# A squared-relu layer by seven block products over chunk pairs, the last stage so for all row pairs, and an issue order from tables

## The chip, the cores and the metric

The kernel runs on one core of one Trainium2 chip. The metric is device microseconds of one execution. Before the change three runs gave 356.97, 357.52 and 357.94; the median is **357.52 us**.

## The reference, cut to what matters

Three layers follow each other on a batch of 2 sequences of 768 rows, 512 features: a local attention with block summaries (8 heads), a mixture of 4 attention experts of which the best 2 count, and a layer with a squared relu and a gate. The change touches the third most:

```python
def _moe2_ref(x, mu_k, mu_r, w_k, w_v, w_r):
    x_prev = np.concatenate([np.zeros((B, 1, D)), x[:, :-1, :]], axis=1)
    xk = mu_k * x + (1.0 - mu_k) * x_prev
    xr = mu_r * x + (1.0 - mu_r) * x_prev
    k = np.maximum(xk @ w_k, 0.0)          # 512 -> 1024, the hidden layer
    v = k * k @ w_v                        # 1024 -> 512
    r = 1.0 / (1.0 + np.exp(-(xr @ w_r)))  # the gate
    return r * v
```

w_k, w_v and w_r come as 64-bit floats, which the chip unpacks from integer words.

## The kernel before

Every matmul of two dense operands is done with operands split into a rounded part and a remainder ("halves"), as three products: rounded x rounded, rounded x remainder, remainder x rounded. Rounding is one instruction of ScalarE, VectorE or GpSimd (`rnd`, lines 699 to 702), the remainder one subtraction of VectorE or GpSimd (`sub`, 707 and 709).

The 1536 rows are worked in 4 chunks of 384 (two for each sequence). Stage 1 (`stage1_*`) is the local attention by tiles of 128 rows; `proj_all` (products of line 1077 and 1095) and `attention` (1177 scores, 1237 transposes, 1263 weighted values, 1305 output projection) are the experts by chunk. Then for the last layer: `mix` makes xk or xr of a chunk in halves (line 1424 is its multiply-add), `rec` is the gate (1442: 12 matmuls of 512 columns for each of 12 row tiles, then Sigmoid at 1451), `hid` the hidden layer (1466: for each chunk 8 groups of 128 hidden columns, each 4 pieces of the contraction x 3 matmuls of 384 columns; then Relu on ScalarE at 1471 and a multiply out of PSUM on VectorE at 1472). The last stage works on tiles of 128 rows. `mono(t)` does one tile by plain block products; `duo(ta, tb)` does two tiles by seven block products (2 x 2 blocks over row tile and hidden half, and hidden half and output half), with sums and differences of the blocks made by VectorE or GpSimd (`add`, 1371 and 1372). Each block product is 12 matmuls of 256 columns (1513). `ALONE = 2` tiles go through `mono`, ten through `duo`. Weights are loaded by `load_wr`, `load_wk`, `load_wv`, each 128 rows through `raw64` (1348 to 1357: two words to one 32-bit float).

The order of all work is set when the program is built. Each instruction, or small group, is an `op` with the tiles that it reads and writes and up to four "ways" (engines). `Plan.run` gives each a rank (its distance to the end by cost formulas, plus an entry of the table `RANKS`), and `Plan.simulate` places them one by one on model clocks of the engines with biases from `LEANS` and `ENGINE_BIAS`; the resulting order is what every engine's queue gets. Tiles come from small pools by name (`x`, `pq0`, `wx`, `stage`, ...), PSUM has six shared banks `ps` and one each of `a1` and `a2`. From the middle on, weight pieces are put into tiles of earlier stages that are done (`parts`).

Of the kernel before, what the change touches and what calls it, by code (L numbers as in the profile page):

```python
# [58 lines left out]
ALONE = 2

RANKS = (
# [1716 lines left out]
```

## Time and profile before

| what | value |
|---|---|
| runs | 356.97, 357.52, 357.94 us |
| span of the profiled execution, first to last instruction | 356.0 us |
| time of the profiled execution beside its span | not recorded apart; the median of the runs is 1.5 us above the span |
| TensorE busy | 340.2 us (96%), 3084 matmuls |
| VectorE busy | 290.5 us (82%), 878 instructions |
| ScalarE busy | 215.6 us (61%), 597 |
| GpSimd busy | 115.9 us (33%), 128 |
| granted TensorE clock | 1.000 |
| DMA | 33.89 MB, mean 95 GB/s |

A busy time is the time in which at least one instruction of the engine runs; instructions of one engine overlap a little, so counts times means are more than busy time. Matmuls are shown with a duration of some twice their pitch, because the next one starts before the last has ended; the pitch is read from unbroken runs.

### The profile page before, as it was taken

How to read it: one execution, taken by the hardware profiler on the slowest of the kernel's cores; microseconds unless marked ns; L12 is line 12 of the kernel's file. 1: busy time of each engine (PE TensorE's matmuls, PEld its weight loads, DVE VectorE, ACT ScalarE, POOL GpSimd, SP SyncE). 2: the span in 40 equal slices, each digit the busy share in tenths (PEclk: the TensorE clock that was granted, in tenths of full speed). 3: DMA queues.
4: the chain of work that ended last, by engine and by line, in shares of the span. 5: the costliest groups of instructions: out<-in, count | busy, mean ns of one | idle time of the engine just before them, and what ended most of it. 6: DMA issues, size and time to landing. Idle time of an engine off the chain costs nothing.

```text
span 356.0 us, 8257 instructions
## 1 busy us (share of the span) xinstructions
PE 340.2 (96%) x3084; PEld 307.2 (86%) x3084; DVE 290.5 (82%) x878; ACT 215.6 (61%) x597; POOL 115.9 (33%) x128
## 2 busy tenths in 40 slices
PE   3979979999999999999999999999999999999996
PEld 2769967888878899888878898999999898999995
DVE  3897778999999899899997799999995266326994
ACT  1888757999888555786678367775740333522440
POOL 0345030034410534445625532063224351601113
PEclk9999999999999999999999999999999999999999
DMA  7997847646130132102211310100002000000112
GB/s 267 384 356 216 286 135 227 225 141 192 46 124 3 59 119 80 40 2 94 84 61 59 101 56 30 53 1 17 29 32 100 5 0 0 2 0 2 59 47 73
DMA packets 19206, 33.89 MB, mean 95 GB/s; under 512 B 2112, under 2 KB 9024, under 8 KB 19168
## 3 DMA queue, kind: packets, MB, share of 16 engines
q1 hardware_dynamic: 19168, 33.38, 28.2%
q8 instruction: 24, 0.39, 0.5%
q14 instruction: 14, 0.11, 0.1%
HBM read 29.63 MB, written 3.15 MB: 92 GB/s over the span
## 4 chain that ended last, share of the span: by engine, by line
PE 61%; DVE 1%; issue 0%
PE ps L1466 19%; PE ps L1513 17%; PE ps L1442 9%; PE ps L1305 4%; PE a L1263 3%; PE ps L1237 3%; PE ps L1077 2%; PE ps L1177 2%; PE ps L1095 2%; DVE kw L707 0%; PE ps L1218 0%; DVE pq L1184 0%; DVE wvgl L1538 0%; DVE wvgl L1371 0%; DVE gl L1102 0%
## 5 line engine op out<-in xcount | busy, mean ns | idle before, releaser
L1197 ACT ACTIVATE pq<-pq,nm 128x128 f32<-128x128 f32 (+5 forms) x48 | 31.7, 661 | 10.6 <-DVE nm L1184 8.6
L1351 POOL TENSOR_SCALAR f<-f 128x512 f32<-128x512 f32 x13 | 23.8, 1834 | 33.1 <-ACT f L1348 31.1
L1077 PE MATMUL ps<-x,wqkh 128*128 128x384 f32 x128 | 34.2, 348 | 0.0
L1184 DVE CUSTOM_DVE_ANT_0 pq<-ps,trm 128x384 f32<-128x384 f32 (+3 forms) x64 | 29.7, 501 | 1.3 <-PE ps L1177 1.3
L944 ACT ACTIVATE pp<-pp,nm 128x120 f32<-128x120 f32 x72 | 27.4, 383 | 0.4 <-DVE nm L941 0.4
L1237 PE MATMUL ps<-cst,pq 128*128 128x128 f32 x168 | 25.0, 275 | 0.0
L1077 PEld LDWEIGHTS ps<-x,wqkh 128*128 128x128 f32 x128 | 22.1, 189 | 0.7
L1095 PE MATMUL ps<-wvgh,x 128*128 128x260 f32 x96 | 21.7, 300 | 0.1
L1077 PE MATMUL ps<-x,wqkl 128*128 128x384 f32 x64 | 21.5, 335 | 0.0
L1466 PE MATMUL ps<-x,wqkh 128*128 128x384 f32 x96 | 21.4, 338 | 0.0
L1237 PEld LDWEIGHTS ps<-cst,pq 128*128 128x128 f32 x168 | 19.5, 141 | 1.9 <-issue 0.9
L1263 PE MATMUL a<-th,vv 128*64 128x384 f32 (+2 forms) x144 | 20.6, 421 | 0.0
L1177 PE MATMUL ps<-ks,q 64*128 64x384 f32 (+3 forms) x192 | 20.3, 338 | 0.0
L1472 DVE SCALAR_TENSOR_TENSOR q<-ps,q 128x384 f32<-128x384 f32 x16 | 8.5, 556 | 13.9 <-ACT q L1471 13.8
L1466 PE MATMUL ps<-x,wqkl 128*128 128x384 f32 x96 | 19.4, 337 | 0.0
L699 ACT ACTIVATE th<-ps 128x384 f32<-128x384 f32 (+1 forms) x37 | 16.7, 482 | 3.8 <-PE ps L1237 2.7
L1442 PE MATMUL ps<-vw,x 128*128 128x512 f32 x72 | 18.7, 395 | 0.0
L1348 ACT ACTIVATE f<-stage 128x512 f32<-128x512 f32 x20 | 13.5, 682 | 8.5 <-DVE th L707 3.0
L1177 PEld LDWEIGHTS ps<-ks,q 64*128 64x128 f32 x192 | 15.1, 185 | 3.9 <-issue 1.0
L1095 PEld LDWEIGHTS ps<-wvgh,x 128*128 128x128 f32 x96 | 16.1, 188 | 1.8 <-issue 1.2
L941 DVE CUSTOM_DVE_ANT_0 pp<-ps,msk 128x120 f32<-128x120 f32 x72 | 15.8, 275 | 1.9 <-PE ps L918 1.8
L1466 PEld LDWEIGHTS ps<-x,wqkh 128*128 128x128 f32 x96 | 17.1, 188 | 0.0
(324 smaller groups left out, 1074.7 us busy)
## 6 DMA issues: line engine op xcount, KB each, us to landing
stage<-in_wk SPq DMA_DIRECT2D x8, 512.0 KB, 3.5
stage<-in_wv SPq DMA_DIRECT2D x8, 512.0 KB, 3.9
qb<-in_qT SPq DMA_DIRECT2D x12, 256.0 KB, 5.0
out_y<-wvgl SPq DMA_DIRECT2D x24, 128.0 KB, 1.7
vw<-in_vp SPq DMA_DIRECT2D x8, 256.0 KB, 4.1
stage<-in_wr SPq DMA_DIRECT2D x4, 512.0 KB
kw<-in_kS SPq DMA_DIRECT2D x6, 320.0 KB
ks<-in_kS SPq DMA_DIRECT2D x4, 400.0 KB, 5.3
```

The source lines that it names most:

```text
L944: op("act", act(NK, True) + 186, lambda i=i, z=z, pr=pr, nm=nm: nc.scalar.activation(pr()[:, i], pr()[:, i], AF.Exp, bias=nm.t[:, i:i + 1] ...
L1077: mm(p.t[:, :C], a.t[:, kc, cols], x.t[:, kc, :], start=(kc == 0 and i == 0), stop=(kc == KC - 1 and i == 2))
L1095: mm(p.t[:, :260], x.t[:, kc, tok], a.t[:, kc, :], start=(kc == 0 and i == 0), stop=(kc == KC - 1 and i == 2))
L1177: mm(ps[e2].t[:, :z - a], q1.t[r, x, tok], ks.t[r, y, a:z], start=n == 0, stop=n == 2)
L1184: nc.vector.tensor_tensor_reduce(pr.t[:, a:z], p.t[:, :z - a], trm.t[:, 512 - nk + a:512 - nk + z] if z == nk and not a else (trm.t[:, 512 ...
L1197: nc.scalar.activation(pr.t[:, :nk], pr.t[:, :nk], AF.Exp, bias=nm.t[:, m:m + 1], scale=-1.0, accum_out=sme.t[:, k, i, 0:1]), r=[nm, (sme, ...
L1237: lambda i=i, kb=kb, pr=pr: nc.tensor.transpose(p.t[:, i * P:(i + 1) * P], pr.t[:, kb * P:(kb + 1) * P], ident()),
L1263: mm(acc.t[64 * e2:64 * e2 + 64, tq0 * P:(tq0 + cnt) * P], vv.t[:, kb, e * D:(e + 1) * D], th[e2].t[:, i0 * P:(i0 + cnt) * P], start=first ...
L1351: ("pool", pool_ts(512), lambda: nc.gpsimd.tensor_scalar(ff(), ff(), F64_TOP, None, ALU.min))],
L1442: mm(p.t, a.t[:, kc, tok], w[2](), start=(kc == 0 and i == 0), stop=(kc == KC - 1 and i == 2))
L1466: mm(p.t[:, :C], w[2]()[:, mo:mo + P], a.t[:, kc, :], start=(kc == 0 and i == 0), stop=(kc == KC - 1 and i == 2))
L1513: mm(p.t[:, :256], x.t[:, u, j * P:(j + 1) * P], v[2]()[:, col:col + 256], start=(at == 0 and i == 0), stop=(at == n - 1 and i == 2))
```

## The change

The hidden layer is done for two chunks at a time (`hid(0)`, `hid(2)`), by the scheme that `duo` had: blocks of the contraction (two halves of the 512 features) and of the rows (two chunks), against blocks of w_k by contraction half and column parity of 256-column pieces. Seven block products take the place of eight; each has four groups of 128 hidden columns with 6 matmuls of 384 columns. Sums and differences of weight blocks are made at load time (`seven`, now shared by w_k and w_v), those of inputs between the products (`into`), those of results after them (`copy`, `plus`, `plus_in`, `more`), and the squared relu follows as its own step on a result in SBUF (`square`). `mono` goes; all twelve row tiles go through `duo` in six pairs, where the first and second product's results are now copied out of PSUM. The gate's steps are the same. Pools are merged by size (`w`, `b6`, `s4`, `t`, ...), all eight PSUM banks are shared. The planner's simulation is gone: `ORDER` is a list of 2151 numbers, entry n issues operation n // 4 done its (n % 4)th way, and `HOMES` gives each tile its slot. The clipping of unpacked weights on GpSimd gets a second operation (times 1.0). Copies of value sums into the value tiles can be done by any engine or by a DMA.

```diff
-RANKS = (
...
-LEANS = {
...
+ORDER = (
+    12, 4, 0, 8, 24, 16, 44, 36, 52, 32, 60, 56, 28, 68, 20, 64, 220, 48, 172, 40, 72, 193, 76, 260, 672, 224, 678,
+    236, 80, 264, 834, 228, 268, 84, 272, 88, 360, 836, 244, 232, 92, 252, 1297, 184, 256, 308, 276, 284, 280, 188,
...
+HOMES = (
+    0, 0, 16, 0, 0, 0, 0, 0, 0, 0, 0, 0, 1, 3, 4, 1, 2, 0, 2, 5, 6, 7, 0, 1, 15, 26, 0, 1, 2, 3, 19, 20, 23, 24, 21,
...
+        assert len(ORDER) == len(self.ops) and len(HOMES) == len(self.bufs)
+        for b, home in zip(self.bufs, HOMES):
+            b.slot = home
+        issued = set()
+        for n in ORDER:
+            o = self.ops[n // 4]
+            assert o.preds <= issued
             for b in o.bufs:
                 if b.tile is None:
                     b.tile = alloc(b)
...
+            o.ways[n % 4][2]()
+            issued.add(o)
...
-    banks = {"ps": 6, "a1": 1, "a2": 1}
+    banks = {"ps": 8}
+    kinds = dict(w=39, u3=5, p1=3, t=8, q=8, b6=10, s4=6)
     slots = dict(
-        cst=1, msk=1, trm=1, mu=1, omu=1, wqkh=1, wqkl=1, wvgh=1, wvgl=1, woh=1, wol=1, x2=3, qb=NQ, kw=2, vw=4,
-        f64=2, oh=1, ol=1, ksm=1, vs=1, x=4, nm=8, sms=1, rss=1, sme=1, rse=1, ks=1, vv=1, q1=2, gl=2, gate=2, cc=1, cnt=1, gsum=1, mx=1,
-        fs=1, pq0=3, pq1=3, pq2=3, nm2=10, wx=8, **SLOTS, **banks,
+        cst=1, msk=1, mu=1, omu=1, ksm=1, ks=1, nm=8, sms=1, rss=1, sme=1, rse=1, gl=2, gate=2, cc=1, cnt=1, gsum=1,
+        mx=1, nm2=10, **kinds, **banks,
     )
-    plan = Plan(slots, ("ps",), banks)
+    plan = Plan(slots, ("ps", *kinds), banks)
     buf, op = plan.buf, plan.op
...
-            if t >= PUT:
-                op("sp", dma(NB * 2048, 255.0), lambda v=v, s2=s2: nc.sync.dma_start(v.t[SROW[s2]], vsm[b].t[:NB]),
-                   r=[vsm[b]], w=[(v, "sum")])
-                continue
...
+                ("sp", dma(NB * 2048, 255.0), lambda v=v, s2=s2: nc.sync.dma_start(v.t[SROW[s2]], vsm[b].t[:NB])),
+            ], r=[vsm[b]], w=[(v, "sum")], issue=850)
...
-                       ("pool", pool_ts(512), lambda: nc.gpsimd.tensor_scalar(ff(), ff(), F64_TOP, None, ALU.min))],
+                       ("pool", pool_ts(512), lambda: nc.gpsimd.tensor_scalar(
+                           ff(), ff(), F64_TOP, 1.0, ALU.min, ALU.mult))],
...
+    def seven(fa, fb, sums, homes):
+        w = [part("q", 256), part("q", 256)] + homes
+        for i, (x, y, fn) in enumerate(sums):
+            both("dve", at(*x), at(*y[:3]), at(*y[3:]), 256, fn, [(fa, 0), (fb, 0), (fa, 1), (fb, 1)][:2 + i // 2],
+                 [(x[0], 1)])
+        halves(w[0], w[1], at(fa, 0, 0), [(fa, 0)], 256)
+        halves(w[2], w[3], at(fb, 0, 0, 512), [(fb, 0)])
+        halves(w[4], w[5], at(fa, 1, 0, 512), [(fa, 1)])
+        halves(w[6], w[7], at(fb, 1, 0, 512), [(fb, 1)])
+        return w
+    def load_wk():
+        cols = wk.rearrange("k (m c) -> k m c", m=2)
+        for n in range(4):
+            g, j = divmod(n, 2)
+            fa, fb = (raw64(cols[k * P:(k + 1) * P, :, 256 * g:256 * g + 256], 2) for k in (j, j + 2))
+            a11, a21, a12, a22 = (fa, 0, 0), (fa, 0, 256), (fb, 0, 0), (fb, 0, 256)
+            s1, s2, s3, s4 = (fa, 1, 0), (fa, 1, 256), (fb, 1, 0), (fb, 1, 256)
+            homes = pieces("s4", 2, 512) if n < 2 else [part("w"), part("w")]
+            homes += [part("w"), part("w")] + [part(("w", "w", "w", "u3")[n]) for x in range(2)]
+            wkp[g, j] = seven(fa, fb, ((s1, a21 + a22, ALU.add), (s2, s1 + a11, ALU.subtract),
+                                       (s3, a11 + a21, ALU.subtract), (s4, a12 + s2, ALU.subtract)), homes)
...
+    def mixed(c, i, kc):
+        piece = part("t", C, F32)
+        mb, mk, tmp = piece
+        def cur():
+            return x2s[c].t[:, kc, 1:]
+        def prv():
+            return x2s[c].t[:, kc, 0:C]
+        rd = [(x2s[c], kc), (x2s[c], "prev"), mu, omu]
+        mul_by("pool", tmp, prv, lambda: omu.t[:, i:i + 1], C, rd, [(mb, mk)])
+        op("dve", dve(C) + 60, lambda: nc.vector.scalar_tensor_tensor(
+            tmp(), cur(), mu.t[:, i:i + 1], tmp(), ALU.mult, ALU.add), r=rd, w=[(mb, mk)], lock=True)
+        return piece
...
+    def blocks(c):
+        if c:
+            return [pieces("b6", 4, C, F32) for i in range(2)]
+        b = buf("ks", [P, FC, C])
+        return [[(b, i, lambda i=i: b.t[:, i]) for i in range(4 * h, 4 * h + 4)] for h in range(2)]
+    def copy(x, p, n):
+        rnd("act", x[2], lambda: p.t[:, :n], n, [p], [x[:2]])
+    def plus(x, p, n):
+        op("dve", dve(n), lambda: nc.vector.tensor_tensor(x[2](), p.t[:, :n], x[2](), ALU.add), r=[p], w=[x[:2]])
+    def hid(c):
+        (c11, c21), (c12, c22) = k2s[c], k2s[c + 1] = blocks(c), blocks(c + 1)
+        b11, b21, b12, b22 = ([mixed(c + cc, kc, kc) for kc in (2 * kh, 2 * kh + 1)]
+                              for cc in range(2) for kh in range(2))
+        def split(x):
+            o = buf("b6", [P, 2, 2, C], F32R)
+            for j in range(2):
+                halves(*((o, (u, j), lambda u=u, j=j: o.t[:, u, j]) for u in range(2)), x[j][2], [x[j][:2]], C)
+            return o
+        def into(dst, x, y):
+            for j in range(2):
+                both("dve", dst[j][2], x[j][2], y[j][2], C, ALU.subtract, [x[j][:2], y[j][:2]], [dst[j][:2]])
+        def product(m, x, w, col):
+            g, o = divmod(m, 2)
+            o = col + o * P
             p = bank("ps")
+            def go():
+                for j in range(2):
+                    h, l = wkp[g, j][2 * w:2 * w + 2]
+                    for i, (a, u) in enumerate(((h, 0), (h, 1), (l, 0))):
+                        mm(p.t[:, :C], a[2]()[:, o:o + P], x.t[:, u, j], start=not (j or i), stop=j == 1 and i == 2)
+            op("pe", 6 * pe_r(C), go, r=[x] + [v[:2] for j in range(2) for v in wkp[g, j][2 * w:2 * w + 2]], w=[p],
+               stream="p3")
+            return p
+        def square(x):
+            any_of("act", [
+                ("dve", dve(C) + 60, lambda: nc.vector.scalar_tensor_tensor(
+                    x[2](), x[2](), 0.0, x[2](), ALU.max, ALU.mult), True),
+                ("act", 2 * act(C, True), lambda: (nc.scalar.activation(x[2](), x[2](), AF.Relu),
+                                                   nc.scalar.activation(x[2](), x[2](), AF.Square))),
+                ("pool", pool_ts(C) + pool_tt(C), lambda: (
+                    nc.gpsimd.tensor_scalar(x[2](), x[2](), 0.0, 1.0, ALU.max, ALU.mult),
+                    nc.gpsimd.tensor_tensor(x[2](), x[2](), x[2](), ALU.mult))),
+            ], w=[x[:2]])
+        def plus_in(dst, p, x):
+            op("dve", dve(C), lambda: nc.vector.tensor_tensor(dst[2](), p.t[:, :C], x[2](), ALU.add), r=[p, x[:2]],
+               w=[dst[:2]])
+        def more(x, y):
+            both("dve", x[2], x[2], y[2], C, ALU.add, [y[:2]], [x[:2]])
+        four = range(4)
+        x = split(b11)
+        for m in four:
+            copy(c11[m], product(m, x, 0, 0), C)
+        into(b11, b12, b11)
+        x = split(b11)
+        for m in four:
+            copy(c22[m], product(m, x, 2, 0), C)
+        into(b11, b22, b11)
+        x = split(b11)
+        for m in four:
+            plus_in(c12[m], product(m, x, 2, 256), c11[m])
+        x = split(b21)
+        for m in four:
+            plus(c11[m], product(m, x, 1, 0), C)
+            square(c11[m])
+        into(b12, b22, b12)
+        x = split(b12)
+        for m in four:
+            plus_in(c21[m], product(m, x, 3, 0), c12[m])
+            more(c12[m], c22[m])
+            more(c22[m], c21[m])
+            square(c22[m])
+        into(b21, b21, b11)
+        x = split(b21)
+        for m in four:
+            plus(c21[m], product(m, x, 1, 256), C)
+            square(c21[m])
+        x = split(b22)
+        for m in four:
+            plus(c12[m], product(m, x, 3, 256), C)
+            square(c12[m])
...
+        (cb, ck, ca), (db, dk, da) = part("u3", dt=F32), part("u3", dt=F32)
+        s, d = (flat(ca), [(cb, ck)]), (flat(da), [(db, dk)])
+        p1 = kept(product(operand(a11), 0, 0))
+        add(s, a21, a22, ALU.add)
+        p5 = kept(product(operand(s), 2, 0))
+        add(s, s, a11, ALU.subtract)
+        u2 = plus_to(product(operand(s), 2, 256), p1)
+        plus(p1, product(operand(a12), 1, 0), 256)
+        result(ta, 0, p1)
+        add(d, a11, a21, ALU.subtract)
+        u3 = plus_to(product(operand(d), 3, 0), u2)
+        more(u2, p5)
+        more(p5, u3)
+        result(tb, 256, p5)
+        plus(u3, product(operand(a22), 3, 256), 256)
+        result(tb, 0, u3)
+        add(s, a12, s, ALU.subtract)
+        plus(u2, product(operand(s), 1, 256), 256)
+        result(ta, 256, u2)
...
+    rg, k2s = [], {}
+    rec(0, mix(0))
+    load_wk()
     attention(3)
+    rec(1, mix(1))
+    hid(0)
+    hid(2)
+    rec(2, mix(2))
+    rec(3, mix(3))
+    load_wv()
+    for t in range(0, B * TPB, 2):
+        duo(t, t + 1)
     plan.run(alloc)
```

## Rows read from the trace of the kernel before

**Rows 1.** Busy us and instructions (x) of each engine in eight stretches, with TensorE clock.
```profile
core 0: us, PE busy (x) PEld busy (x) DVE busy (x) ACT busy (x) POOL busy (x), PEclk, DMA share, GB/s
0.00:20.00 20.00, 12.52 (x275) 10.36 (x276) 12.32 (x63) 11.31 (x49) 4.54 (x15) 1.00 0.93 334
20.00:60.00 40.00, 35.35 (x505) 31.31 (x503) 32.62 (x142) 29.55 (x111) 12.06 (x14) 1.00 0.72 230
60.00:120.00 60.00, 60.00 (x750) 49.20 (x750) 58.44 (x236) 54.31 (x188) 15.18 (x18) 1.00 0.38 121
120.00:177.00 57.00, 56.88 (x421) 50.47 (x417) 52.06 (x154) 34.55 (x87) 27.50 (x30) 1.00 0.23 75
177.00:241.00 64.00, 64.00 (x364) 57.70 (x361) 59.20 (x141) 44.77 (x90) 22.83 (x19) 1.00 0.15 50
241.00:272.40 31.40, 31.40 (x267) 31.40 (x266) 28.59 (x58) 14.95 (x28) 9.36 (x8) 1.00 0.11 36
272.40:322.70 50.30, 50.30 (x267) 47.17 (x266) 21.39 (x39) 15.70 (x31) 16.99 (x18) 1.00 0.03 10
322.70:356.00 33.30, 29.77 (x253) 29.56 (x251) 25.91 (x54) 10.44 (x18) 7.47 (x8) 1.00 0.14 48
sum 356.00, PE 340.21 PEld 307.16 DVE 290.53 ACT 215.59 POOL 115.94; mean PE 42.53 PEld 38.40 DVE 36.32 ACT 26.95 POOL 14.49
```

**Rows 2.** Chain that ended last: start us, length us, engine, tile, line, count.
```profile
224.37 16.83 PE ps L1466 x96
241.20 31.21 PE ps L1513 x264
272.41 8.33 PE ps L1442 x36
...
352.50 0.43 DVE wvgl L1538
...
352.96 0.42 DVE wvgl L1371
```

**Rows 3.** All products of two lines: the hidden stage's, then the last stage's.
```profile
...
187.40:322.80 135.40, 68.75 (x384) 67.10 (x383) 1.00 0.10 32
...
0.00:356.00 356.00, 61.29 (x516) 61.22 (x516) 1.00 0.29 95
```

**Rows 4.** Timeline of TensorE (start, length): products that follow four transposes at 147.04.
```profile
147.39 0.42 PE L1305 MATMUL ps<-oh,woh 128*128 128x384 f32 x1
147.65 0.34 PE L1305 MATMUL ps<-ol,woh 128*128 128x384 f32 x1
```

**Rows 5.** Four kinds of VectorE instructions: duration ns, least/median/most.
```profile
L1424 DVE SCALAR_TENSOR_TENSOR ol<-x,mu,ol x24: 603/608/1373, 207.7 to 301.6; 128x384 f32<-128x384 f32 x24
...
L1355 DVE SCALAR_TENSOR_TENSOR f<-stage,f x20: 678/684/1462, 67.5 to 228.6; 128x512 int32<-128x512 int32 x20
...
L707 DVE TENSOR_TENSOR x<-ol,x x19: 544/550/1112, 210.2 to 305.1; 128x384 fp32r<-128x384 f32 x19
L707 DVE TENSOR_TENSOR f<-wx,f x8: 676/681/689, 247.8 to 346.7; 128x512 fp32r<-128x512 f32 x8
```

**Rows 6.** Timeline of VectorE: two instructions that follow each other.
```profile
204.64 0.43 DVE L1371 TENSOR_TENSOR f<-f,f 128x256 f32<-128x256 f32 x1
204.98 0.42 DVE L700 CAST wx<-f 128x512 fp32r<-128x512 f32 x1
```

**Rows 7.** Groups by line and shape: busy us, mean ns, idle before.
```profile
L1424 DVE SCALAR_TENSOR_TENSOR ol<-x,mu,ol 128x384 f32<-128x384 f32 x24 | 15.3, 654 | 2.1 <-POOL ol L716 2.1
L707 DVE TENSOR_TENSOR f<-wx,f 128x512 fp32r<-128x512 f32 x8 | 5.5, 682 | 0.0
...
L1351 POOL TENSOR_SCALAR f<-f 128x512 f32<-128x512 f32 x13 | 23.8, 1834 | 33.1 <-ACT f L1348 31.1 <-DVE nm L1184 1.9
...
L1451 ACT ACT_TABLE_LOAD x1 | 1.3, 1283 | 0.0
```

**Rows 8.** Waits of TensorE before 60 us: us, times, longest.
```profile
PE ps L923 <- DMA ks<-in_kS: 5.0, 1, 5.0
PE a L1002 <- ACT ks L699: 2.3, 1, 2.3
```

More of the change, by code (lines that the diff above doesn't have):

```diff
@@ L381 @@
 class Op:
[L382 to L383 removed]
+    pass
 class Plan:
[L395 to L402 removed]
@@ L403 @@
-    HOLD = dict(pe=200.0, act=225.0, dve=200.0, pool=135.0, sp=1150.0)
-    TICK, BUSY = 10240.0 / 3, 3060.0
-    MODES = ("full", "rows", "half", "quarter")
-    SWITCH = {}
-    for a in MODES:
-        for b in MODES:
-            SWITCH[a, b] = 95.0
     def __init__(self, slots, shared, banks):
         self.slots, self.shared, self.banks = slots, shared, banks
-        self.ops, self.order, self.chain = [], {p: [] for p in slots}, {}
-        self.n, self.tilt = 0, 0.0
+        self.ops, self.order, self.bufs, self.chain = [], {p: [] for p in slots}, [], {}
@@ L417, in buf, with op @@
     def buf(self, pool, shape, dt=F32):
-        self.n += 1
-        b = Buf(pool, shape, dt, f"{pool}_{self.n}")
+        b = Buf(pool, shape, dt, f"{pool}_{len(self.bufs) + 1}")
+        self.bufs.append(b)
         self.order[pool].append(b)
         return b
-    def op(self, eng, cost, fn, r=(), w=(), stream=None, late=0.0, bias=0.0, claim=(), ways=(), mode="full", lock=False):
+    def op(self, eng, cost, fn, r=(), w=(), stream=None, late=0.0, claim=(), ways=(), mode="full", lock=False, issue=0):
@@ L424, in op @@
         o = Op()
-        o.tilt = self.tilt
         o.ways = [(*w, w[0] == "pool")[:4] for w in [(eng, cost, fn, lock or eng == "pool")] + list(ways)]
-        o.lock = o.ways[0][3]
-        o.eng, o.cost, o.fn, o.seq, o.late = eng, cost, fn, len(self.ops), late
+        o.eng, o.seq, o.late, o.issue = eng, len(self.ops), late, issue
         o.prev, o.stream, o.mode = None, stream, mode
-        if stream:
-            bias += BIAS.get(stream, 0.0)
-        o.preds, o.succs, o.bufs, o.prio, o.start, o.end = set(), [], [], bias, None, None
+        o.preds, o.bufs = set(), []
@@ L455, in op @@
         return o
-    def lag(self, a, e):
-        return a.late + self.LAG[a.eng][e]
     def run(self, alloc):
-        for o in self.ops:
-            if o.prev is not None and o.prev not in o.preds:
-                o.preds.add(o.prev)
-            else:
-                o.prev = None
-            o.need = len(o.preds)
-            for p in o.preds:
-                p.succs.append(o)
-            for b in o.bufs:
-                b.left += 1
-                if b.first is None:
-                    b.first = o
-        extra = {}
-        for pool, bufs in self.order.items():
-            if pool in self.shared or pool == "stage":
-                continue
-            n = self.slots[pool]
-            for i in range(n, len(bufs)):
-                old = bufs[i - n].users
-                for o in old:
-                    extra.setdefault(o.seq, []).append(bufs[i].first)
-        for o in reversed(self.ops):
-            far = 0.0
-            for s in o.succs + extra.get(o.seq, []):
-                if s.seq > o.seq:
-                    far = max(far, s.prio + (0.0 if s.prev is o else self.lag(o, s.eng)))
-            o.prio += far + o.cost
-        assert len(RANKS) == len(self.ops)
-        for o, d in zip(self.ops, RANKS):
-            o.rank = round(o.prio) + d
-            o.lean = [b + (o.tilt if w[0] == "dve" else 0.0) for w, b in zip(o.ways, LEANS.get(o.seq, (0, 0, 0, 0)))]
-            o.eng, o.cost, o.fn, o.lock = o.ways[0]
-        done = self.simulate()
-        assert done is not None, "no operation can be placed"
-        for o in done:
+        assert len(ORDER) == len(self.ops) and len(HOMES) == len(self.bufs)
[5 more added lines that the diff above has]
+            assert o.preds <= issued
             for b in o.bufs:
@@ L1432, in rec @@
         x_h, x_l = x
-        rg3 = [rg[(c * TPC + tq) % 6] for tq in range(TPC)]
+        rg3 = [part("w", dt=F32) for tq in range(TPC)]
+        rg.extend(rg3)
         for tq in range(TPC):
@@ L1493, in operand @@
     def operand(x):
[L1494 removed]
+        o = buf("s4", [P, 2, 512], F32R)
         h, l = ((o, i, lambda i=i: o.t[:, i].rearrange("p (a b) -> p a b", a=4)) for i in range(2))
@@ L1513, in go @@
                         mm(p.t[:, :256], x.t[:, u, j * P:(j + 1) * P], v[2]()[:, col:col + 256],
-                           start=(at == 0 and i == 0), stop=(at == n - 1 and i == 2))
+                           start=not (j or i), stop=j == FC // 2 - 1 and i == 2)
             op("pe", 12 * pe_r(256), go, r=[x] + [v[:2] for j in range(FC // 2) for v in wvp[j][2 * w:2 * w + 2]],
                w=[p], stream="p3")
-        for k, term in enumerate(terms):
-            part(k, *term)
-        return p
@@ new lines, in kept, with plus_to, more, result @@
+        def kept(p):
+            x = part("t", 256, F32)
+            copy(x, p, 256)
+            return x
+        def plus_to(p, y):
+            x = part("t", 256, F32)
+            op("dve", dve(256), lambda: nc.vector.tensor_tensor(x[2](), p.t[:, :256], y[2](), ALU.add), r=[p, y[:2]],
+               w=[x[:2]])
+            return x
+        def more(x, y):
+            both("dve", x[2], x[2], y[2], 256, ALU.add, [y[:2]], [x[:2]])
+        def result(t, col, x):
+            rb, rk, ra = rg[t]
+            row = t * P
+            both("dve", x[2], x[2], lambda: ra()[:, col:col + 256], 256, ALU.mult, [(rb, rk)], [x[:2]])
+            op("sp", dma(P * 1024), lambda: nc.sync.dma_start(out[row:row + P, col:col + 256], x[2]()), r=[x[:2]])
@@ L1700, in attn_moe_rwkv @@
-    for b_ in sum(plan.order.values(), []):
-        b_.users = []
-    for o in plan.ops:
-        for b_ in o.bufs:
-            b_.users.append(o)
+    rg, k2s = [], {}
+    rec(0, mix(0))
+    load_wk()
+    attention(3)
+    rec(1, mix(1))
[6 more added lines that the diff above has]
+        duo(t, t + 1)
     plan.run(alloc)
```

448 lines of the change are left out of this document (90 added, 358 removed), and 430 rows, old and new, of tables (HOMES, LEANS, ORDER, RANKS).

## The prediction

> **What bounds the kernel now.** I read the stretches first, then the chain, then the groups of instructions. The stretch table [rows 1] says who is full: TensorE is busy 60.00 of 60 us from 60 to 120, 56.88 of 57, 64.00 of 64, 31.40 of 31.4, 50.30 of 50.3, and 29.77 of the last 33.3. From 60 us to its last instruction it lost 0.12 us, at a granted clock of 1.00 (2.4 GHz) in every stretch. All that is not TensorE's work is 12.1 us of idle time before 60 us (7.5 in the first 20, while the keys land) and 3.5 us after the last product. The chain [rows 2] ends as a plain row of product groups, and its last links are one VectorE add (0.43) and one multiply (0.42) before the last store. So the time is: idle at the start + TensorE's work + tail. A product that goes is worth its whole pitch, as long as no other engine becomes late.
>
> The next engine is VectorE: 58.44 of 60 us from 60 to 120 and 59.20 of 64 from 177 to 241, but 21.39 of 50.3 from 272 to 323 [rows 1]. The back part of the kernel has VectorE time to spare; the change lives there.
>
> **Part 1: TensorE.** The hidden product took 4 chunks x 8 column groups x 4 x 3 = 384 matmuls of 384 columns; with seven block products for each of two chunk pairs it takes 2 x 7 x 4 groups x 6 = 336. An unbroken run of 96 lasts 16.83 us, 0.1753 each [rows 2]; so 48 fewer are -8.4 us. The last stage was two single row tiles (48 each) and five pairs (84 each), 516 of 256 columns, which stand beside the 384 in [rows 3]; six pairs are 504. 264 took 31.21 us, 0.118 each [rows 2]: -1.4 us. The gate products (144 of 512 columns), projections and attention keep their counts. Sum: **-9.8 us**.
>
> A change from one shape of product to another costs a little: three products of 384 columns follow four transposes, and the second starts 0.26 us after the first where 0.175 is usual [rows 4], so 0.085 for a return from transposes. I counted both orders (before from the trace, after from the new table): returns from transposes to full products go from 35 to 43 (+0.7 us), all changes that involve half, quarter or row-split products from 78 to 63 (-1.3 us at the same price). I take 0, with -1.4 and +0.7 as ends.
>
> **Part 2: VectorE, ScalarE, GpSimd.** Each hidden group was one Relu on ScalarE and one VectorE multiply from PSUM (32 + 32). Now 56 groups each leave PSUM once: 16 copies, 40 VectorE adds; then 32 squarings, 16 adds between blocks, 16 subtractions of inputs, and 28 operand splits (rounding + remainder) where 16 were. The weights get 16 small sums and 16 splits instead of 8 of full width. What matters is where it lies and on which engine, which the new table fixes: entry n is operation n/4 done its (n mod 4)th way. I counted VectorE's part of it from the first hidden product to the end. Durations are the medians of [rows 5], and 0.42 for 256 columns [rows 2], less the 0.08 by which consecutive VectorE instructions overlap (one of 0.43 at 204.64 is followed at 204.98 [rows 6]):
> - 78 of 512 columns at 0.60: 46.8
> - 97 of 384 at 0.47: 45.6
> - 73 of 256 at 0.335: 24.5
> - 17 mixing multiplies at 0.525 and 20 unpacking steps of weights at 0.51 (two of the kind shown at 0.60, one cheaper): 19.1; three others 0.8
>
> Sum 136.8 us. TensorE in the same stretch: 336 x 0.1753 + 90 gate products x 0.231 (36 in 8.31 us) + 21 x 0.1753 + 504 x 0.118 = 142.9 us. So VectorE is asked for 96% of TensorE's time where before it had 135 us in the 179 after 177 us (75%) [rows 1]. ScalarE comes to 109 us (all 32 squarings are on it, two passes each at 0.52), GpSimd to 28.
>
> Does 96% cost TensorE anything? Bound below: 0, since from 60 to 120 VectorE ran at 97% and TensorE lost nothing [rows 1]. Bound above: if VectorE can be filled only to 92%, as from 177 to 241, it needs 136.8 / 0.92 = 148.7, which is 5.8 us more than TensorE. Taken in slices of some 10 us of TensorE's work along the table's order, VectorE's tally exceeds TensorE's in a few (11.1 against 10.4 where the second pair's last products meet the gate products, 10.9 against 10.4 at the end of the fourth attention), 1.6 us in all, and what is late there is the next operand's split. I take **+2 us**: near the lower end, because the row with the fuller VectorE lost nothing and the higher bound's row did not lose anything either; it only shows a lower filling.
>
> **Part 3: pools, tables, start.** Merged pools and fixed homes add no instruction. GpSimd's clipping of weights gets a second operation; the old form took 1834 ns [rows 7], the new one is not shown. Between nothing and twice that, it falls on an engine that is idle for two thirds of the span and before the weights are due: 0. The writes of value sums, 12 DMAs of 16 before, are 6 in the table, the rest on engines. Before 60 us TensorE lost 5.0 us to the first key load and, from 20 to 60, 4.6 us to small waits, the longest 2.3 us at the products of probabilities with values [rows 1, 8]. Another order can save these 4.6 or lose as much; the loads are the same. I take 0. Before 177 us the table asks VectorE for less than before (138 against some 155 us), so I see no new bound there. The tail (one add, one multiply, one store) is unchanged.
>
> **Sum.** Span 356.0 - 9.8 + 2 = 348.2; the runs' median is 357.52, 1.5 us above the profiled span, and I carry that: **349.7 us**.
>
> **Rivals.**
> A (forecast). TensorE stays the bound, VectorE just keeps up: 349.7; own range 347 to 352.5. Chance 0.61.
>
> B. VectorE becomes the bound of the last 145 us, because each operand split and each addition out of PSUM passes it, and a product can't start before its split. For: 96% in the tally, and no stretch of before held 96% for longer than 60 us. Against: the table's sums are level, no slice over 107%. Price 5.8 for 2: 353.5. Chance 0.17.
>
> C. The new order also removes the small waits between 20 and 60 us: 4.6 less, 345.1. For: they are waits for banks and value sums, and banks and value-sum writes are just what is changed there. Against: the first 30 us are loads, and these stay. Chance 0.12.
>
> D (slower). GpSimd and VectorE block each other. The place is the hidden products and the last stage, where VectorE's two-input instructions run back to back; if it had to wait out all of GpSimd's 28 us, it would need 136.8 + 28 = 165, 22 more than TensorE: 370. It decides from the point where more than 16 of the 28 us block (142.9 + 9.8 - 136.8), 57%. For: the mixing multiply has median 608 and maximum 1373 ns [rows 5]. Against: its mean is 654 [rows 7], 46 ns over its median, so its 24 instructions lost 1.1 us in all, and the remainders of the last stage have mean 682 and median 681 [rows 5, 7]. At 46 ns on each of the 17 multiplies and half of some 170 others with two inputs in SBUF it would be 4.7 us, which is inside B. Chance 0.07.
> The Trainium skill (SBUF — State Buffer, "SBUF: two separate sides") has the port pair shared by VectorE and GpSimd as an exclusive lock held for a whole instruction, the loser blocked. By that rule alone every overlap with a two-input VectorE instruction is serialised, rival D's full price; the maxima agree with it, the means say that such meetings are rare.
>
> E (it does not do what it says). ScalarE's Square needs another function table than Sigmoid and Relu. A table load took 1283 ns [rows 7]; two for each of 32 squarings are 82 us on ScalarE, 191 against 142.9: about 396. Against: one load at the first Sigmoid served Relu, Copy, Abs and Sigmoid until the end; it is the second of two in [rows 7]. Chance 0.03.
> The Trainium skill (ScalarE: Activation LUTs, "Table sets: the hidden batching unit") says that cheap functions such as relu, copy, identity and abs are in every set; it does not list square there, and no run here shows one.
>
> **How the numbers follow.** Differences under 0.3% (1.1 us) can't be told from none. A, C and most of B are faster: 0.61 + 0.12 + 0.14 = 0.87. The rest of B is about no change: 0.04; D and E, less a little of D, are slower: 0.09. Range: the low end takes in C (345.1, here 345), the high end reaches through B (352 to 355), leaving out D, E and the edges of B and C, some 0.18.
>
> **What would show it.** Right: 336 hidden matmuls still at 0.175 us pitch, 504 in the last stage, TensorE busy 330 us (340.2 - 9.8), idle after 60 us of 1 to 4 us, all of it behind VectorE (operand splits or additions from PSUM); VectorE over 90% in every stretch after the first hidden product; one table load beyond the first. Wrong: TensorE idle over 5 us in that stretch (B, or D where VectorE instructions are lengthened beside GpSimd's), idle before 60 us away from 12 us by more than 3 (C or its opposite), or more table loads (E). The prediction fails altogether if the order makes TensorE wait in the attention part, between 60 and 177 us, where I expect nothing.

## The result, and the profile after

The changed kernel takes **346.56 us** (median of 4 runs, 345.94 to 347.84) against 357.25 of the kernel before beside it (4 runs): ratio 0.970, 95% interval 0.967 to 0.974. Forecast were 349.7 and a range of 345 to 355. The profiled execution took 346.9 us, its span 345.1. One execution in experiment 4, of 555.83 us at a mean granted clock of 0.567, is left out of its median.

The stretches of the changed kernel, with the columns of [rows 1]; the first four are the same stretches. The first hidden products run at 195.5 us among gate products, from 207.7 to 265 they run alone, then come gate products to 284, and from 281 the last stage:

```profile
0.00:20.00 20.00, 12.60 (x304) 10.74 (x304) 12.44 (x74) 11.06 (x50) 5.02 (x14) 1.00 0.94 328
20.00:60.00 40.00, 38.10 (x560) 34.77 (x553) 37.82 (x146) 34.27 (x125) 19.74 (x23) 1.00 0.83 273
60.00:120.00 60.00, 60.00 (x693) 52.92 (x694) 56.25 (x215) 53.46 (x173) 29.36 (x32) 1.00 0.37 116
120.00:177.00 57.00, 56.44 (x426) 45.88 (x422) 53.88 (x170) 36.62 (x95) 25.08 (x29) 1.00 0.09 29
177.00:200.00 23.00, 23.00 (x132) 18.19 (x131) 22.83 (x51) 16.93 (x38) 2.37 (x2) 1.00 0.21 69
200.00:231.00 31.00, 31.00 (x175) 30.61 (x175) 30.31 (x60) 26.63 (x57) 10.98 (x9) 1.00 0.06 18
231.00:268.00 37.00, 35.25 (x194) 33.70 (x193) 36.08 (x72) 31.41 (x69) 11.92 (x10) 1.00 0.17 57
268.00:285.00 17.00, 17.00 (x89) 14.42 (x88) 16.89 (x34) 15.79 (x33) 1.89 (x2) 1.00 0.01 1
285.00:345.10 60.10, 56.47 (x476) 56.16 (x474) 56.97 (x117) 35.95 (x72) 17.15 (x11) 1.00 0.16 54
sum 345.10, PE 329.86 PEld 297.40 DVE 323.47 ACT 262.14 POOL 123.51; mean PE 36.65 PEld 33.04 DVE 35.94 ACT 29.13 POOL 13.72
```

Stretch length less TensorE's busy time is its idle time. The two spans differ by 10.9 us, and this is where the difference lies:

| | before | after | difference | forecast |
|---|---|---|---|---|
| TensorE busy | 340.21 | 329.86 | -10.35 | -9.8 |
| idle before 60 us | 12.13 | 9.30 | -2.8 | 0 |
| idle 60 us to the last product | 0.12 | 2.31 | +2.2 | +2 |
| behind the last product | 3.53 | 3.63 | +0.1 | 0 |

The second column to read is VectorE's: 56.25 of 60, 53.88 of 57, then 97 to 99% in each stretch up to the last product. Before it was 59.20 of 64, 28.59 of 31.4 and 21.39 of 50.3 there [rows 1].

The chain that ends last still consists of long rows of products at the old pitch (15.72 / 90 = 0.175, 52.74 / 444 = 0.119; 0.1753 and 0.118 in [rows 2]), with pieces of VectorE's work between them:

```profile
207.72 15.72 PE ps L1174 x90
...
246.31 1.62 DVE t L1100 x2
...
284.48 52.74 PE ps L1261 x444
```

TensorE's waits in the changed kernel (us, times, longest). The first is the keys, 6.5 where it was 5.0 [rows 8]; the two of L1174 make up 1.6 of its 1.75 us of idle time between 200 us and the last product, both behind VectorE:

```profile
PE ps L589 <- DMA ks<-in_kS: 6.5, 1, 6.5
PE ps L668 <- DVE w L370: 1.3, 2, 1.0
PE ps L1174 <- DVE ks L1147: 1.0, 1, 1.0
...
PE ps L1174 <- DVE b L1192: 0.6, 1, 0.6
```

What goes before the wait at 236 us is seen on two timelines (start, length), VectorE's and then GpSimd's at the same time. VectorE's last three instructions here last 1.12, 1.37 and 1.09 us where such ones take 0.68, 0.55 and 0.61, 1.7 us longer in all. The one before them, which reads PSUM, runs beside GpSimd at its usual 0.55.

```profile
228.97 0.55 DVE L1147 TENSOR_TENSOR ks<-ps,ks 128x384 f32<-128x384 f32 x1
229.43 1.12 DVE L377 TENSOR_TENSOR w<-s,w 128x512 fp32r<-128x512 f32 x1
230.47 1.37 DVE L1036 TENSOR_TENSOR t<-t,t 128x384 f32<-128x384 f32 x1
231.77 1.09 DVE L1100 SCALAR_TENSOR_TENSOR t<-b,mu,t 128x384 f32<-128x384 f32 x1
```

```profile
227.26 2.73 POOL L1037 TENSOR_TENSOR b<-b,ks 128x384 f32<-128x384 f32 x2 [5.04 <-DVE b L1036]
229.97 1.46 POOL L379 TENSOR_TENSOR b<-t,b 128x384 fp32r<-128x384 f32 x1
231.62 0.83 POOL L379 TENSOR_TENSOR q<-s,q 128x256 fp32r<-128x256 f32 x1 [0.19 <-ACT q L369]
```

ScalarE's groups of the squaring and its loads of function tables: 32 squarings at 0.526 us, and two loads in all, as before.

```profile
L1185 ACT ACTIVATE b<-b 128x384 f32<-128x384 f32 x24 | 12.6, 526 | 0.8
...
L1185 ACT ACTIVATE ks<-ks 128x384 f32<-128x384 f32 x8 | 4.2, 526 | 0.3
...
L369 ACT ACT_TABLE_LOAD x1 | 1.3, 1283 | 8.9 <-DMA ks<-in_kS 8.9
L1132 ACT ACT_TABLE_LOAD x1 | 1.3, 1283 | 0.0
```

### The profile page after: what moved, and what is told of

Read it like the earlier page. It is cut to its first block, busy times and chain, and to the rows that moved or that the text cites. A ratio compares the mean times of both kernels' runs of the same rounds, so it can differ in the third digit from the quotient of the medians.

```text
span 345.1 us, 8336 instructions
## 1 busy us (share of the span) xinstructions
PE 329.9 (96%) x3024; PEld 297.4 (86%) x3024; DVE 323.5 (94%) x928; ACT 262.1 (76%) x703; POOL 123.5 (36%) x131
## 4 chain that ended last, share of the span: by engine, by line
PE 77%; DVE 16%; DMA 2%; ACT 2%; issue 1%; SPq 0%; POOL 0%; DVEq 0%; POOLq 0%
PE ps L1261 16%; PE ps L1174 14%; PE ps L1123 10%; PE ps L743 6%; PE ps L929 5%; PE ps L843 5%; PE ps L903 4%; PE ps L761 4%; PE ps L971 3%; PE ps L650 2%; PE ps L584 2%; PE ps L668 2%; DMA ks<-in_kS 2%; DVE b L370 1%; DVE ksm L487 1%; DVE t L1100 1%
## 5 line engine op out<-in xcount | busy, mean ns | idle before, releaser
L1261 PE MATMUL ps<-w,s 128*128 128x256 f32 x336 | 48.9, 281 | 0.0
L1261 PEld LDWEIGHTS ps<-w,s 128*128 128x128 f32 x336 | 44.0, 188 | 0.2
L1174 PE MATMUL ps<-b,w 128*128 128x384 f32 x216 | 41.6, 339 | 1.8 <-DVE ks L1147 1.0
L1174 PEld LDWEIGHTS ps<-b,w 128*128 128x128 f32 x216 | 38.0, 188 | 2.8 <-DVE ks L1147 1.3
L743 PE MATMUL ps<-b,w 128*128 128x384 f32 x192 | 39.2, 348 | 0.0
L1123 PE MATMUL ps<-w,b 128*128 128x512 f32 x144 | 35.9, 398 | 0.0
L369 ACT ACTIVATE t<-ps 128x384 f32<-128x384 f32 (+1 forms) x53 | 23.3, 464 | 13.2 <-PE ps L903 8.4
L743 PEld LDWEIGHTS ps<-b,w 128*128 128x128 f32 x192 | 32.3, 188 | 1.1 <-issue 0.2
L1123 PEld LDWEIGHTS ps<-w,b 128*128 128x128 f32 x144 | 26.5, 188 | 5.6 <-issue 0.3
L610 ACT ACTIVATE w<-w,nm 128x120 f32<-128x120 f32 x72 | 27.5, 383 | 0.8 <-DVE nm L607 0.5
L369 ACT ACTIVATE b<-ps 128x384 f32<-128x384 f32 (+4 forms) x46 | 22.1, 488 | 4.2 <-PE ps L668 2.4
L369 ACT ACTIVATE s<-u 128x512 fp32r<-128x512 f32 x24 | 14.9, 627 | 8.7 <-PE ps L1261 5.2
L971 PE MATMUL ps<-u,w 128*128 128x384 f32 x96 | 21.1, 349 | 0.0
L1100 DVE SCALAR_TENSOR_TENSOR t<-b,mu,t 128x384 f32<-128x384 f32 x32 | 20.9, 671 | 0.2
```

Source lines behind the costliest of these rows:

```text
L369: ways = [("act", act(n, sb), lambda: nc.scalar.activation(dst(), src(), AF.Copy)), ("dve", dve2(n) if sb else dve(n), lambda: nc.vector.t ...
L610: op("act", act(NK, True) + 186, lambda i=i, z=z, pr=pr, nm=nm: nc.scalar.activation(pr()[:, i], pr()[:, i], AF.Exp, bias=nm.t[:, i:i + 1] ...
L743: mm(p.t[:, :C], a[kc].t[:, cols], x.t[:, kc, :], start=(kc == 0 and i == 0), stop=(kc == KC - 1 and i == 2))
L971: mm(p.t[:, :C], a[ep].t[:, m * P:(m + 1) * P], x.t[:, ep, :], start=(ep == 0 and i == 0), stop=(ep == 1 and i == 2))
L1100: op("dve", dve(C) + 60, lambda: nc.vector.scalar_tensor_tensor(tmp(), cur(), mu.t[:, i:i + 1], tmp(), ALU.mult, ALU.add), r=rd, w=[(mb, m ...
L1123: mm(p.t, a.t[:, kc, tok], w[2](), start=(kc == 0 and i == 0), stop=(kc == KC - 1 and i == 2))
```

## The experiments

Ratios are to runs of the kernel before on the same chip (medians 356.5 to 357.0 us), with their 95% intervals. Open were: does a removed product really bring its pitch, had VectorE any room left, what does GpSimd's help cost, and where do the 2.8 us of the start come from?

**1. The products alone.** The kernel before, less 60 matmuls.

```
  for i, (w, a) in enumerate(((w_h, x_h), (w_h, x_l), (w_l, x_h))):
+     if i == 1 and (kc == 3 or kc == 2 and mo < 256):
+         continue
...
+     if len(terms) > 1 and i == 1 and at < 6:
+         continue
```

> The kernel before, with 60 of its matmuls left out (in each chunk's hidden products 12 of 96, in the third products of the two single row tiles 6 of 16 each) and every instruction of the other engines kept in place. Theory 1 (the removed products carry the gain, at their pitch): 48 x 0.1753 + 12 x 0.118 = 9.8 us less, 347.4 against 357.25, TensorE busy 330. Rival (TensorE's row is full because it is paced by what surrounds it, and the gain came from the new order): less than 5 us of gain, the rest turns into idle time of TensorE.

352.47 us, ratio 0.987 (0.984 to 0.989): 4.2 us less, not 9.8. The old order has TensorE wait between 177 and 272 us, where it never did [rows 1]; the stretches and waits of this run:

```profile
177.00:241.00 64.00, 61.30 (x351) 54.29 (x350) 60.06 (x137) 43.79 (x87) 23.32 (x19) 1.00 0.16 50
241.00:272.40 31.40, 30.42 (x244) 29.53 (x243) 28.73 (x59) 12.77 (x25) 10.15 (x10) 1.00 0.12 40
```

```profile
PE ps L1517 <- POOL f L709: 1.1, 1, 1.1
...
PE ps L1442 <- DVE x L707: 1.0, 1, 1.0
...
PE ps L1517 <- ACT fs L699: 0.7, 1, 0.7
```

Of the 9.8 us some 3.7 became idle time there. TensorE's busy time is 332.82 us, 2.4 above the 330.4 expected; its mean granted clock from 20 to 60 us is 0.96, and whether that is all of the 2.4 is open. So the rival is right for that order: TensorE's full row hid operands that were only just in time. The reverse, the changed order with as many matmuls as before, was not run.

**2. TensorE's work out of the changed kernel.** Of the six matmuls of every hidden product the four that use a remainder go.

```
- for i, (a, u) in enumerate(((h, 0), (h, 1), (l, 0))):
-     mm(p.t[:, :C], a[2]()[:, o:o + P], x.t[:, u, j], start=not (j or i), stop=j == 1 and i == 2)
+ mm(p.t[:, :C], h[2]()[:, o:o + P], x.t[:, 0, j], start=j == 0, stop=j == 1)
```

> The changed kernel with the two remainder matmuls of each hidden product left out (224 of 336, 39.2 us of TensorE); all copies, additions, splits and squarings stay. Theory A, as forecast (TensorE is the bound, VectorE needs 136.8 us against TensorE's 142.9, plus 2 us of loss that is VectorE's): 4 to 8 us less than the changed kernel's 346.6, then VectorE is the bound: 338.6 to 342.6. Theory B (VectorE with its lengthened instructions already is the bound of the last 145 us): 0 to 3 us less. TensorE alone as the bound: 39 us less, 307.

347.91 us, ratio 0.974 (0.972 to 0.976): nothing gained for 39 us of TensorE. From 200 to 268 us VectorE is as full as before, TensorE idles 23.5 of the 68 us, and its granted clock falls to a mean of 0.74 and 0.68, part of the time at the 1.2 GHz level:

```profile
200.00:231.00 31.00, 22.34 (x82) 17.62 (x80) 30.62 (x61) 26.61 (x58) 11.24 (x9) 0.74 0.05 18
231.00:268.00 37.00, 22.14 (x65) 16.55 (x66) 36.08 (x73) 31.24 (x69) 13.56 (x10) 0.68 0.17 57
```

**3. More VectorE work in the changed kernel**, and **4. the same in the kernel before.**

```
  nc.vector.tensor_tensor(x[2](), p.t[:, :n], x[2](), ALU.add)
+ if n == C:
+     nc.vector.tensor_tensor(x[2](), x[2](), x[2](), ALU.max)
...
  nc.vector.scalar_tensor_tensor(ka(), p.t[:, :C], 0.0, ka(), ALU.max, ALU.mult)
+ if m % 4:
+     nc.vector.tensor_tensor(ka(), ka(), ka(), ALU.max)
```

> The changed kernel with 24 more VectorE instructions of 384 columns (a maximum of a tile with itself, two inputs in SBUF) right behind 24 of its additions out of PSUM in the hidden products: 24 x 0.47 = 11.3 us more for VectorE. Theory A (6 us of room on VectorE in the last 145 us, less the 2 us already lost): 5 to 8 us slower than the changed kernel, 351.6 to 354.6. Theory B (VectorE is the bound already): 10 to 12 us slower, 356.6 to 358.6. TensorE alone as the bound: no more than 1 us slower.

> The kernel before with the same 24 VectorE instructions of 384 columns (a maximum of a tile with itself, 0.47 us each, 11.3 us in all) behind 24 of the multiplies of its hidden products. Theory 1 (on record: VectorE has room in the back part before the change, 135 us of work in 179): no more than 1 us slower, and with the changed kernel's +17 for the same 24 this shows that the change used the room up. Rival (room doesn't travel: where the hidden products lie VectorE was busy 59.2 of 64 us, so some 5 us fit and the rest waits): 4 to 7 us slower.

After: 363.43 us, ratio 1.016 (1.013 to 1.019), 16.9 us slower than 346.56. Before: 364.53, ratio 1.021 (1.018 to 1.024), 7.5 us slower. The 11.3 us of the expectations were too little: the 24 instructions have a median of 0.56 us, and with those that were lengthened take 15.5 us after the change and 16.2 in the kernel before.

VectorE's busy time from the first hidden product to the end shows what became of it, first in the changed kernel, then with the 24 instructions (314 for 290), which are L1150 there:

```profile
195.50:345.10 149.60, 144.21 (x952) 138.99 (x950) 144.76 (x290) 112.68 (x232) 41.94 (x31) 1.00 0.12 40
```

```profile
194.50:359.20 164.70, 150.00 (x953) 142.67 (x951) 159.69 (x314) 113.43 (x232) 41.72 (x31) 0.96 0.11 36
```

```profile
L1150 DVE TENSOR_TENSOR b<-b 128x384 f32<-128x384 f32 x16 | 10.3, 644 | 0.5
...
L1150 DVE TENSOR_TENSOR ks<-ks 128x384 f32<-128x384 f32 x8 | 5.2, 651 | 0.3
```

VectorE is busy 14.9 us longer, and that stretch is 15.1 us longer: all of it passes to the end, as theory B has it, at a higher price than its 10 to 12. The profiled execution (361.04 us) is one of the shorter ones; where the others lose up to 3.2 us more isn't seen. TensorE idles 5.7 and 5.4 us in two stretches, its granted clock sinks to a mean of 0.91 and 0.80 there, and in the whole run it is busy 5.0 us longer (334.87 for 329.86) with the same matmuls; since VectorE's row alone is as long as the loss, these runs don't show that the clock added to it.

```profile
231.00:268.00 37.00, 31.30 (x164) 30.33 (x164) 36.55 (x67) 27.22 (x60) 11.77 (x9) 0.91 0.09 29
268.00:285.00 17.00, 11.62 (x40) 8.35 (x39) 16.80 (x36) 9.78 (x20) 2.00 (x2) 0.80 0.18 63
```

In the kernel before about half of the added time found room, so theory 1 falls and the rival holds, a little above its 4 to 7 us. Where it fitted is told by the stretches: from 272 to 323 us, where half of that order's hidden products run, VectorE is busy 7.5 us more and TensorE waits for nothing; from 177 to 272 us TensorE, which never idled there, is idle for 5.0 us.

```profile
177.00:241.00 64.00, 62.03 (x341) 54.87 (x340) 60.02 (x136) 40.41 (x81) 18.58 (x17) 0.97 0.16 50
241.00:272.40 31.40, 28.41 (x232) 28.00 (x231) 31.23 (x58) 16.24 (x32) 8.80 (x8) 1.00 0.06 22
272.40:322.70 50.30, 50.30 (x282) 47.17 (x281) 28.87 (x57) 14.70 (x29) 19.92 (x21) 1.00 0.06 19
```

**5. GpSimd's share given to VectorE.**

```
+ if at >= 1500 and way[0] == "pool":
+     way = next((w for w in o.ways if w[0] == "dve"), way)
```

> The changed kernel with the 31 operations that GpSimd does behind the first hidden products (sums, remainders, two clips, one multiply) done by VectorE in their places; alone they would take VectorE about 12.4 us at 0.34 to 0.60 each. Theory L (each meeting with GpSimd lengthens VectorE's two-input instructions, 6.2 us in all by the excess of their means over their shortest; that goes with GpSimd): net about +6 us for VectorE, so 6 to 8 us slower than the changed kernel's 346.6, and L1100, L377 and L1036 come back to 0.61, 0.55 to 0.60 and 0.55. Theory N (the excess is something else): 12 to 15 us slower, the means stay. Rival D of the forecast (blocked for nearly all of GpSimd's time, here 42 us of busy time): faster than the changed kernel.

350.9 us, ratio 0.982 (0.979 to 0.985): 4.3 us slower than the changed kernel. The groups of three kinds of VectorE instructions behind 200 us (busy us, mean ns), first in the changed kernel, then without GpSimd, where line numbers are 3 higher:

```profile
L1100 DVE SCALAR_TENSOR_TENSOR t<-b,mu,t 128x384 f32<-128x384 f32 x17 | 11.6, 703 | 0.1
...
L1036 DVE TENSOR_TENSOR t<-t,w 128x256 f32<-128x256 f32 x18 | 8.2, 476 | 0.0
L1147 DVE TENSOR_TENSOR b<-ps,b 128x384 f32<-128x384 f32 x16 | 8.2, 547 | 0.0
```

```profile
L1103 DVE SCALAR_TENSOR_TENSOR t<-b,mu,t 128x384 f32<-128x384 f32 x17 | 10.0, 610 | 0.0
L1039 DVE TENSOR_TENSOR t<-t,w 128x256 f32<-128x256 f32 x24 | 9.6, 425 | 0.0
...
L1150 DVE TENSOR_TENSOR b<-ps,b 128x384 f32<-128x384 f32 x16 | 8.5, 546 | 0.0
```

The means come down to about the shortest durations, but that of L1147, which has one input in PSUM, doesn't move. From the first hidden product to the end VectorE does the same 290 instructions as in the changed kernel and the 31 taken over:

```profile
194.50:348.30 153.80, 146.14 (x952) 139.16 (x951) 150.50 (x321) 112.27 (x232) 0.00 (x0) 1.00 0.12 39
```

It is busy 150.50 us for 144.76, 5.7 more, though the work taken over is 12.4 us (estimated from the durations); so 12.4 - 5.7 = 6.7 us of its time in the changed kernel was lengthening. GpSimd was busy 41.9 us there to relieve it by 5.7. That is theory L, which had 6.2 us of lengthening and about 6 us net for VectorE; the run's 4.3 us are below its 6 to 8.

**6 and 7. VectorE's work out of the changed kernel**, then TensorE's too.

```
- both("dve", x[2], x[2], y[2], C, ALU.add, [y[:2]], [x[:2]])
+ any_of("dve", [("dve", dve(C), lambda: None, True), ("pool", pool_tt(C), lambda: None)], r=[y[:2]], w=[x[:2]])
...
+ if j == 0 and i == 1:
+     continue
```

> The changed kernel with the 16 additions between blocks in the hidden products left out (13 on VectorE, 13 x 0.47 = 6.1 us, and 3 on GpSimd). Theory B (VectorE and TensorE are both at their floor in the back part): only the idle time that TensorE has there can go, 1.6 to 1.75 us less, 344.8 to 345.0. Rival (VectorE alone is the bound, as leaving out 39 us of TensorE without any gain could also be read): 5 to 6 us less.

> As the run before it (16 additions left out, 6.1 us of VectorE), and one of the six matmuls of each hidden product left out too (56 x 0.1747 = 9.8 us of TensorE). Theory B (two floors at the same height, and both have come down): 6 to 8 us less than the changed kernel's 346.6, about 339.5. Rival (a third bound right under the two, as ScalarE with 31.4 of 37 us, or the order itself): 2 to 4 us less, with waits behind ScalarE.

345.69 us (0.968; 0.966 to 0.971) and 342.33 (0.960; 0.958 to 0.963): 0.9 and 4.2 us less than 346.56; the first, as its interval overlaps that of the changed kernel, isn't told from none by the medians. From 231 to 268 us, the first and then the second of the two:

```profile
231.00:268.00 37.00, 36.67 (x204) 35.65 (x203) 33.67 (x67) 33.02 (x72) 10.01 (x8) 1.00 0.17 57
```

```profile
231.00:268.00 37.00, 33.73 (x174) 30.43 (x174) 35.69 (x73) 33.51 (x73) 9.07 (x7) 1.00 0.16 57
```

With VectorE relieved TensorE is the full row (0.33 us idle for 1.75); with TensorE relieved as well VectorE is the fuller one again. So both bounds stood at one height. The second gain is below the 6 to 8 expected (5.3 between the profiled spans, 339.8 for 345.1): one wait of 1.1 us behind ScalarE joins those behind VectorE, as its rival said, though most are VectorE's (3.2).

**8 and 9. Two attempts at a better back part.** Three roundings go from VectorE to ScalarE and one multiply from GpSimd to ScalarE; in the other kernel work for the last stage is issued later.

```
- 6365 ... 6125 ... 6085 ... 6444
+ 6364 ... 6124 ... 6084 ... 6446
```

```
  in the table: 7297, 7272, 7281 behind 6396; 7612, 7676 behind 6784; 7304 behind 6684; 1453, 1613 behind 1429
```

> The changed kernel with three roundings of hidden operands moved from VectorE to ScalarE (0.27 us each) and one mixing multiply from GpSimd to ScalarE (2.3 us on GpSimd, 0.6 on ScalarE). Theory B (VectorE sets the pace of the hidden products, with its lengthened instructions): 0.8 to 1.5 us less than 346.6, out of the 1.75 us that TensorE idles between 231 and 268 us. Rival (ScalarE, busy 31.4 of 37 there, becomes late in VectorE's place): 0, or up to 1 us slower, with waits behind ScalarE.

> The changed kernel with the same operations on the same engines, some issued later: the two copies of key maxima behind the copies for which TensorE waits at 46 us; of VectorE's work for the last stage two weight remainders and a sum behind the additions out of PSUM at 236 us, and two sums of last-stage operands behind those at 249 us; one of GpSimd's weight remainders behind its next operand's remainder. Theory local (the 1.0 and 0.6 us that TensorE waits at 236 and 249 us are local: VectorE was held there by 1.9 and 1.0 us of lengthening beside GpSimd): both waits go and none comes, 1.6 us less in the back and about 1 in the start, 344.0 against 346.6. Theory floor (VectorE's whole work from the first hidden product on is as long as TensorE's, so what is put off is late further on): the waits at 236 and 249 go or shrink, and as much idle time comes between 250 us and the end; 0 to 1 us less.

346.82 us (0.971; 0.968 to 0.974), no gain: the waits of 1.0 and 0.6 us stand, since the work taken away lay before 231 us (29.59 us busy from 200 to 231 for 30.31) and VectorE is as full behind it. And 348.35 (0.978; 0.976 to 0.981), 1.8 us slower: those two waits are gone or small, and new ones come behind:

```profile
PE ps L1117 <- DVE b L371: 1.0, 1, 1.0
...
PE ps L1168 <- DVE b L1141: 0.6, 1, 0.6
```

Theory floor, though it had 0 to 1 us less: what VectorE puts off is late further on. No version with all its work that was run beats the changed kernel.

**10 to 12. The start.** One key maximum of the kernel before issued later; the mask loaded earlier and two copies issued later in the changed kernel; all its value sums written by DMA.

```
+ late = [done[at.index(s)] for s in (254, 255)]
+ to = done[at.index(311)]
```

```
- 16, 44, 36, 52, 32, 60
+ 16, 32, 44, 36, 52, 60
- 1453, 949, 1560, 1613 ... 1429
+ 949, 1560 ... 1429, 1453, 1613
```

```
- o.ways[n % 4][2]()
+ o.ways[3 if o.issue else n % 4][2]()
```

> The kernel before, with one key maximum of the second batch (the 768-column reduction at 45.49 us, for which VectorE stood 2.49 us waiting for its keys) issued behind the next two remainders on VectorE, and the following load of keys behind it. Theory 1 (the longest small wait of the start, 2.25 us of TensorE at 47.14, is a wait for a bank whose last reader stood behind that reduction; it is an accident of the order, and it passes whole to the end): 1.2 to 2.3 us less, and the wait at 47 us is gone or under 1 us. Rival (the keys' late load is the limit, what needs the reduction is late next): 0 to 0.5 us, and the wait shows up again within the next 15 us.

> The changed kernel with two moves in its start: the first mask is loaded before the third and fourth block of keys, as in the kernel before, so that the first two blocks share the queues with less; and two copies of key maxima on VectorE stand behind the two copies of transposed probabilities for which TensorE waits at 46 us. Theory S (each wait passes whole to the end): the first key wait goes from 6.5 to 5.0 and the 1.3 us at 46 go; 2.0 to 2.8 us less than 346.6. Rival R (the start is bound by the loads as a whole, small waits are given back behind): 0 to 0.7 us less.

> The changed kernel with all 16 writes of value sums into the value tiles made by DMA (6 of them were; the kernel before has 12), in their places of the order. Theory S (what the change gained before 60 us came from writing ten of them by an engine instead of the late DMA queue): the small waits of the start come back at the products of probabilities with values, 1 to 3 us slower than 346.6. Rival R (it came from the shared banks and the order; the start's idle time, 8.6 to 9.6 us in four executions of this order, only scatters): within 0.5 us of 346.6.

The first: 357.75 us (1.002; 1.001 to 1.004), 1.0 us above the kernel before: no gain. The wait of 2.25 us at 47 us is gone from the trace, but that isn't shown to be the move's doing. The kernel of experiment 1 has the same start as the kernel before, and its trace lacks the wait; that of experiment 4 has it at 0.7:

```profile
PE a L1002 <- ACT ks L699: 0.7, 1, 0.7
```

The second: 346.77 (0.971; 0.968 to 0.974), no gain. The 1.3 us at 46 went down to 0.5, while the keys landed no earlier (L589 waited 6.7 us), so why they come later than in the kernel before stays open; it isn't the mask. The third: 358.57 (1.004; 1.001 to 1.007), 12.0 us slower; TensorE waits for those DMAs, and the clock sinks with it (25 to 30 and 50 to 60 us):

```profile
PE ps L668 <- DMA w<-w: 8.8, 3, 4.6
```

```profile
25.00:30.00 5.00, 1.67 (x26) 1.51 (x28) 0.00 (x0) 0.94 (x4) 2.83 (x5) 0.57 0.63 173
...
50.00:60.00 10.00, 5.26 (x77) 4.84 (x78) 3.23 (x9) 2.62 (x6) 4.05 (x6) 0.65 0.57 193
```

This table has no time for such writes; whether they also cost the old order its start was not tried.

## Why the prediction was right, point by point

- **Part 1** (-9.8): right, -10.35 at unchanged pitches; the half us more lies within the ends given for changes of shape. That a removed product is worth its whole pitch hung on a condition, that no other engine becomes late. In the old order it doesn't hold: there the same 60 brought 4.2.
- **Part 2** (+2, "VectorE just keeps up"): the size came out (+2.2, every wait of note behind VectorE) by luck, for the picture was wrong. I read room from 0 to 5.8 us out of 96%. There was none: 39 us less of TensorE brought nothing, and 14.9 us more of VectorE's time made the stretch 15.1 us longer. Rival B's mechanism at rival A's price. The tally of VectorE's own work was close, 150.50 - 12.4 = 138.1 us for 136.8. The term that I mis-sized is GpSimd's toll on VectorE: put at 1 to 4.7 us inside B, measured at 6.7, and in the sum at nothing. With it VectorE is busy 144.76 of the last 149.6 us. That this comes out only 2 us above TensorE's need is how the two happened to stand, not a reserve.
- **"The back part of the kernel has VectorE time to spare"**: true of one place only. From 272 to 323 us [rows 1], where half of the old order's hidden products run, 7.5 us more fitted in without a wait; from 177 to 272 added work made TensorE idle for 5.0 (experiment 4). The change asks for more than that place had.
- **Part 3, the start** (0): the step that failed, by -2.8 us between the two profiles, and the largest part of the forecast's error. The wait of 2.25 us at the products of probabilities with values [rows 8] and most small ones went, the key wait grew by 1.5: a share of rival C, and the result, 346.56, lies between C's 345.1 and A's own range from 347. How much of it lasts is less sure, for the profiled execution of the kernel before was a long one: its span is 356.0 where the median of 54 others, run beside the experiments, is 354.5. The changed kernel's four have a median of 344.75; of the 9.75 us between them 8.05 are the other three rows of the table above, so an estimated 1.7 is left for the start, and 0.3 more lies outside the spans (2.1 to 2.2 us before, 1.8 after). Seven executions with the new order up to 60 us idle 8.6 to 11.1 us there (mean 9.8), three with the old order 9.0 to 12.1 (mean 10.6), only 0.8 apart. What caused this part stays open: no run singled out the shared banks or the order.
- Two smaller readings of Part 3 were off. VectorE is busy 160.4 us before 177 us, not less than before (155.4) as the tally of 138 had it. And TensorE is idle for 0.56 us between 120 and 177 us, where nothing was expected.
- **Rival D**: right to be small. GpSimd lengthened VectorE by 6.7 us, where more than 16 would have decided. The Trainium skill (SBUF — State Buffer, "SBUF: two separate sides") has the shared ports as an exclusive lock, which on VectorE's side an instruction with two inputs in SBUF takes; the trace agrees as to the kind, with the lengthening on instructions of that kind (L1100 703 ns for 610) and not on those that read PSUM (L1147 547 for 546).
- **Rival E**: fell; one load at the first Sigmoid served Square too.
- GpSimd's two-operation clip takes 1.96 us on average where the old one took 1.83 [rows 7], and nothing waits for it.
